# A copy moved from VectorE to ScalarE, and a row maximum issued two key tiles sooner, in an attention kernel

## The chip, the cores and the metric

The kernel runs on one core of a Trainium2 chip. The metric is the device time of one execution in microseconds. Before the change it is 3565.64 us, the median of three runs (3565.61 to 3567.53).

The engines go by short names: PE is TensorE's matrix multiplication and PEld its loading of weights, DVE is VectorE, ACT is ScalarE, POOL is GpSimd, and SP is SyncE, which here issues nearly all DMAs. A bank is one of the eight banks of PSUM, each 128 partitions by 512 fp32 values.

## The reference

Two layers, one after the other and with the same weights. Each layer is an attention block and a block of dense layers, both on a layer-normalised input and added back to it:

```python
def _A_ref(x, wqkv, wo):           # B = 1, S = 2048, D = 640, H = 32, Dh = 20
    qkv = (x @ wqkv).reshape(B, S, 3, H, Dh).transpose(2, 0, 3, 1, 4)
    q, k, v = qkv[0], qkv[1], qkv[2]
    scores = jnp.einsum("bhqd,bhkd->bhqk", q, k) * (Dh ** -0.5)
    p = _softmax(scores, axis=-1)
    o = jnp.einsum("bhqk,bhkd->bhqd", p, v)
    return o.transpose(0, 2, 1, 3).reshape(B, S, D) @ wo
...
x = x + _A_ref(_layernorm(x, axis=-1), A_wqkv, A_wo)
x = x + _B_ref(_layernorm(x, axis=-1), B_w1, B_b1, B_w2, B_b2)   # squared relu of x @ w1 + b1, times w2, + b2
```

The second pair of lines is repeated once. The change touches the softmax over the 2048 keys (its maximum) and the product with the values.

## The kernel before

A layer is three stages: the projections to queries, keys and values (`qkv`), the attention (`attention`), and the output projection with the dense layers. The change lies in the attention.

**Blocks and tiles.** The 32 heads form 8 groups of four, the 2048 queries four parts of 512. A group and a part make a block `t`, 32 blocks to a layer (`NBLK`), numbered from 0. For a block, the keys are gone through in 16 key tiles of 128 (`NKT`). For each key tile and head, `score` (L582) multiplies the keys with the 512 queries into a bank (L591), and ACT takes the exponential into SBUF (L598). `pv` (L600) then multiplies the four heads' exponentials with the values (L603) and adds the result up in bank 7 over the block's 16 tiles. The values carry a column of ones, so the sum of the exponentials comes out beside the result.

**The maximum.** The exponential needs each query's maximum over all keys beforehand. So the scores are also computed the other way round, queries on the partitions, for a later block: `smax` (L489) multiplies 128 queries of one head with 512 keys (L481), and DVE reduces the bank to one column of a small tile `mx` (L493). `smax_half` (L506) does it for two heads at once with 256 keys each: it writes one half of a bank for one head and, after a one-element memset `done_t` on DVE (L512) that serves as a mark, the other half for the other head; DVE reduces both at once (L516). The two halves of the 512 keys go to two columns of `mx`, `c` and `c + 4`, so that a block treated in this way has eight columns for each head and each 128 queries. `two_columns` (L500) has POOL fill the last four with a very small number first, as not every set of keys is done in halves.

When all maxima of block `t` are there (`t` is in the set `over`), `mrows_max` (L549) reduces the columns to one negated maximum (L551), `mrows` (L559) transposes it on DVE (L562), splits it in two parts on POOL (L271 and L276) and stores these to HBM by two DMAs (`d_m`); `mrows_load` (L569) reads them by two DMAs into two extra rows of the query tile `q_t[t]`, so that the score matmul subtracts the maximum.

**The order of the work** is written out by hand. `ORDERS` (L984) holds strings of letters; for nearly all of the attention it is `ubmbanawV` for each key tile: `a` and `b` are score matmuls of even and odd heads (two of each to a tile, in four banks that take turns), `m` and `n` maxima by 512 keys, `u` and `w` the two writes of a bank in halves, `V` the product with the values, for the tile before the one whose scores the string has just issued. Maxima take banks 4, 5 and 6 in turn. Each engine works through its instructions in the order in which `op` (L1088) issues them. So on PE, `w` waits for the mark of `u`, and `V` stands behind `w`; on DVE each tile has the mark, the reductions of `m` and `n`, and then that of `w`. What is issued right after `V` stands behind `w`'s reduction on DVE, and on ACT behind the four exponentials of the scores that were just issued.

`V` of the last tile of a block (tile 15) calls `finish` (L611): DVE copies bank 7 to SBUF (L616), four DMAs store the sums to HBM (`d_s`), and later steps, spread over the next block's tiles by `split`, load them again (`few`), take the reciprocals on POOL (L647), spread them by DMA (`d_r`), multiply and split the result on POOL (L658, L271, L276) and store it. The next block's first `V` starts bank 7 anew and must wait for the copy.

Each `V` also looks whether the next block's maximum is due (L1134): it must be in `over`, its queries must be loaded, and `state["begun"]`, the number of the key tile whose scores were last begun, must have come to `(t - 2) * NKT + 4`. That is the `V` of tile 3, two blocks before the block that needs it. The two loads follow when `begun` is two tiles further. Near the end of an attention the maxima become complete later than that, and the block's maximum is issued when they are.

In the last block no maxima are left, and `both_heads` (L1139) takes the exponentials of two heads in one instruction of 1024 columns (L1160).

Of the kernel before, what the change touches and what calls it, by code (L numbers as in the profile page):

```python
# [8 lines left out]
F32 = mybir.dt.float32  # L9
# [7 lines left out]
P = 128  # L17
# [10 lines left out]
NKT = S // P  # L28
# [5 lines left out]
NBLK = NG * NQB  # L34
# [5 lines left out]
def tile_layers(  # L40
# [11 lines left out]
    nc = tc.nc  # L52
# [3 lines left out]
    small = ctx.enter_context(tc.tile_pool(name="small", bufs=4))  # L56
# [6 lines left out]
    def name(p):  # L63
        n_alloc[0] += 1
        return f"{p}{n_alloc[0]}"

    def slot(shape, dtype, label):
        return arena.tile(shape, dtype, tag="slot", name=name(label))

    def dma(eng, dst, src):  # L70

        if dst.dtype == F32R:
            dst = dst.bitcast(F32)
        if src.dtype == F32R:
            src = src.bitcast(F32)
        eng.dma_start(dst, src)  # L76
# [177 lines left out]
    def split_to(dst_hi, dst_lo, src):  # L254

        nc.scalar.copy(dst_hi, src)
        nc.vector.tensor_sub(dst_lo, src, dst_hi.bitcast(F32))
# [12 lines left out]
    def pool_hi(dst, src):  # L270
        nc.gpsimd.tensor_copy(dst, src)  # L271
# [31 lines left out]
    def after(later, earlier, reason="one half of the rows adds to the bank that the other half has left"):  # L303
        tc.add_manual_dep(
            later.ins,
            earlier.ins.name,
            mybir.DependencyInfo(mybir.DependencyClass.Sync, mybir.DependencyReason.DATA),
            reason=reason,
        )
# [113 lines left out]
    k_t, q_t, v_t, mx_t, kept = {}, {}, {}, {}, {}  # L423
# [46 lines left out]

    def maxima(t):
        if t not in mx_t:
            mx_t[t] = small.tile([P, 4, 4, 8], F32, tag="mx", bufs=14, name=name("mx"))
            if t in PARTLY:
                nc.vector.memset(mx_t[t][:, :, :, :4], LEAST)
        return mx_t[t]

    def by_queries(dst, t, p, sub, c, par, keys=slice(0, QB)):

        b = 64 * par  # L480
        return nc.tensor.matmul(  # L481
            dst,
            q_t[t][b : b + 60, p, sub * P : (sub + 1) * P],
            k_t[t // NQB, c][b : b + 60, p, keys],
            start=True,
            stop=True,
        )
# [6 lines left out]
            maxima(t)[:, 2 * par + p, sub, c : c + 1], dst, axis=AX.X, op=ALU.max  # L494
        )

    halved = set()
    done_t = cpool.tile([1, 1], F32, name="done_t")

    def two_columns(t):  # L500

        if t not in halved:
            halved.add(t)
            nc.gpsimd.memset(maxima(t)[:, :, :, 4:], LEAST)

    def smax_half(bank, t, p, sub, c, half, par, earlier=None):  # L506

        w = QB // 2
        dst = bank[:, par * w : (par + 1) * w]
        m = by_queries(dst, t, p, sub, c, par, slice(half * w, (half + 1) * w))  # L510
        if earlier is None:
            mark = nc.vector.memset(done_t, 0.0)  # L512
            after(mark, m)
            return mark
        after(m, earlier, "matmuls on two halves of the rows write to one bank in turn")
        nc.vector.tensor_reduce(  # L516
            maxima(t)[:, p : p + 3 : 2, sub, c + 4 * half],
            bank.rearrange("q (r k) -> q r k", r=2),
            axis=AX.X,
            op=ALU.max,  # L520
        )
# [27 lines left out]
    def mrows_max(t):  # L549
        nm = nms[t % 2]  # L550
        nc.vector.tensor_reduce(  # L551
            nm[:, :16].rearrange("p (h s) -> p h s", h=4),
            mx_t.pop(t)[:, :, :, : 8 if t in halved else 4],
            axis=AX.X,
            op=ALU.max,
            negate=True,
        )
# [53 lines left out]
    def finish(t, acc):  # L611


        g, qb = divmod(t, NQB)
        o = slot([P, 2, QB], F32, "o")
        nc.vector.tensor_copy(o[:, 0, :], acc)  # L616
        res = []

        def store(q):
            ot = res.pop().rearrange("p l t -> p (l t)")  # L620
            for h in range(4):
                r0 = (4 * g + h) * DH
                dma(q, d_o[r0 : r0 + DH, qb], ot[32 * h : 32 * h + DH])

        if t == NBLK - 1:

            def invert():
                dst = ps_all("rs")
                nc.tensor.matmul(dst, sums_t, o[:, 0, :], start=True, stop=True)
                nc.vector.reciprocal(o[:, 1, :], dst)  # L630

            def divide():
                nc.vector.tensor_mul(o[:, 0, :], o[:, 0, :], o[:, 1, :])
                res.append(slot([P, 2, QB], F32R, "ot"))
                split_to(res[0][:, 0, :], res[0][:, 1, :], o[:, 0, :])

            return [invert, divide, lambda: store(nc.scalar)]

        few = small.tile([P, 16], F32, tag="few", bufs=2, name=name("few"))
        for h in range(4):  # L640
            dma(nc.sync, d_s[t, h : h + 1], o[32 * h + DH : 32 * h + DH + 1, 0, :])

        def load():
            dma(nc.sync, few, d_s[t].rearrange("h (q j) -> (h q) j", j=16))

        def invert():
            nc.gpsimd.tensor_tensor(few, few, minus_t, op=ALU.pow)  # L647

        def spread():
            dma(nc.sync, d_r[t].rearrange("h (q j) -> (h q) j", j=16), few)  # L650

        def gather():
            for h in range(4):
                dma(nc.sync, o[32 * h : 32 * h + 32, 1, :], d_r[t, h].partition_broadcast(32))

        def divide():
            ot = slot([P, 2, QB], F32R, "ot")
            nc.gpsimd.tensor_mul(o[:, 0, :], o[:, 0, :], o[:, 1, :])  # L658
            pool_hi(ot[:, 0, :], o[:, 0, :])
            pool_lo(ot[:, 1, :], o[:, 0, :], ot[:, 0, :].bitcast(F32))  # L660
            res.append(ot)

        return [load, invert, spread, gather, divide, lambda: store(nc.sync)]
# [328 lines left out]
    def attention(first, x_src, first_rows):  # L992
# [7 lines left out]
        state = {"begun": -1, "done": 0, "acc": None, "debt": 0}  # L1000
# [22 lines left out]
        over = {t for t in range(NBLK) if t not in ends and t not in done}  # L1023
# [64 lines left out]
        def op(o):  # L1088
            if o in "ab":
                par = "ab".index(o)  # L1090
                i, p = divmod(st_n[par], 2)
                if i >= last:
                    return
                st_n[par] += 1
                if i > state["begun"]:
                    state["begun"] = i
                    begin(i)
                score(i // NKT, i % NKT, 2 * p + par, es_of.setdefault(i, {}))
            elif o in "mn":
                par = "mn".index(o)  # L1100
                if full[par] or next_pair(full):
                    x = full[par].pop(0)
                    smax(sm_ring, *x, par)
                    turn.append(turn.pop(0))
                    did(x[0])
            elif o == "u":
                if parts or next_pair(parts):
                    x = parts.pop(0)
                    bank = turn.pop(0)
                    opened.append((bank, x, smax_half(banks[:, bank, :], *x, 0)))  # L1110
            elif o == "w":
                if opened:
                    bank, x, mark = opened.pop()
                    smax_half(banks[:, bank, :], *x, 1, mark)
                    turn.append(bank)
                    did(x[0])
            else:
                i = state["done"]
                if i >= last or i < last - NKT and min(st_n) < 2 * (i + 1):
                    return  # L1120
                t, u = divmod(i, NKT)
                if u == 0:
                    state["acc"] = banks[:, 7, :]
                pv(state["acc"], t, u, es_of.pop(i))
                state["done"] += 1
                if u == NKT - 1:
                    steps = finish(t, state["acc"])
                    split.update((i + j, f) for j, f in zip((4, 6, 7, 9, 11, 12), steps))
                t = rows["next"]
                if rows["at"] is not None:  # L1130
                    if state["begun"] >= rows["at"]:
                        mrows_load(t)
                        rows.update(next=t + 1, at=None)
                elif t in over and t in q_t and state["begun"] >= (t - 2) * NKT + 4:  # L1134
                    mrows_max(t)
                    mrows(t)
                    rows["at"] = state["begun"] + 2
# [39 lines left out]
        for o in "abab":  # L1177
            op(o)
# [376 lines left out]
```

## Time and profile before

| what | us |
|---|---|
| median of the three runs | 3565.64 |
| the profiled execution itself | 3565.74 |
| its span, first to last instruction | 3563.6 |
| attention of the first layer, first to last product with the values | 312.8 to 1384.8 |
| attention of the second layer | 2083.7 to 3156.1 |
| PE busy | 3543.9 |
| DVE busy | 2789.1 |
| ACT busy | 2626.9 |

The granted clock of TensorE is 1.000 for the whole span. A row of the timeline gives the start and the length in us, the engine, the line, the operation, what it writes and reads with the shapes, and how many such instructions in sequence the row sums up; in brackets stands the idle time of that engine just before, with what ended it. An instruction on DVE or ACT starts before the one ahead has quite ended, so the time from start to start is shorter than the length. A group's row ends with its total, the mean length in ns, and the idle time before it by what ended it. The stretch of a few tiles around the end of block 8 of the first layer is taken as the example throughout.

### The profile page before, as it was taken

The page shows a single profiled execution, that of the slowest core. Times are in us where ns is not written, and L with a number is a line of the kernel's source. Part 1 is how long each engine was busy: PE and PEld are TensorE (multiplying, and loading weights), DVE is VectorE, ACT ScalarE, POOL GpSimd, SP SyncE. Part 2 cuts the span into 40 slices and gives each one's busy share as a digit, 9 for nine tenths or more (in the row PEclk, how much of TensorE's full clock was granted, in tenths as well). Part 3 has the DMA queues.
Part 4 walks back from the last instruction along what each step waited for, and adds up shares of the span by engine and source line. Part 5 has one row for each costly group of instructions (what it writes and reads, how often), then busy time and mean ns, then how long its engine had stood idle before and what let it go on. Part 6 is the DMA issues. An engine that isn't in the chain of part 4 may idle for free.

```text
span 3563.6 us, 70654 instructions
## 1 busy us (share of the span) xinstructions
PE 3543.9 (99%) x26544; PEld 2153.9 (60%) x26544; DVE 2789.1 (78%) x6069; ACT 2626.9 (74%) x5146; POOL 811.2 (23%) x927
## 2 busy tenths in 40 slices
PE   9999999999999999999999999999999999999999
PEld 7896444444444446999988964444444444469998
DVE  8878999999999993455567789999999999924443
ACT  3778999999999995122237789999999999942221
POOL 6531444211211211111153201211211211211110
PEclk9999999999999999999999999999999999999999
DMA  9775555323211136734487652232232111366221
GB/s 307 273 233 167 170 157 157 105 70 81 57 46 51 46 103 207 255 103 113 135 272 246 197 150 71 62 82 62 64 81 56 50 45 40 116 218 244 74 82 37
DMA packets 377412, 452.76 MB, mean 127 GB/s; under 512 B 176642, under 2 KB 223746, under 8 KB 377070
## 3 DMA queue, kind: packets, MB, share of 16 engines
q1 hardware_dynamic: 376254, 445.89, 41.2%
q8 instruction: 208, 3.41, 0.4%
q10 hardware_dynamic: 816, 2.36, 0.2%
q14 instruction: 134, 1.10, 0.1%
HBM read 273.83 MB, written 174.30 MB: 126 GB/s over the span
## 4 chain that ended last, share of the span: by engine, by line
PE 91%; DVE 5%; DMA 1%; issue 1%; ACT 1%; POOL 0%; SPq 0%; DVEq 0%; ACTq 0%; POOLq 0%
PE banks L603 26%; PE banks L481 22%; PE banks L293 13%; PE banks L591 11%; PE banks L1321 9%; PE banks L331 9%; DVE mx L493 2%; DVE mx L516 1%; DVE o L616 1%; DMA q<-d_qk 1%; SPq L76 0%; DVE bst L244 0%; ACT e L598 0%; PE banks L1153 0%; ACT e L1160 0%
## 5 line engine op out<-in xcount | busy, mean ns | idle before, releaser
L598 ACT ACTIVATE e<-banks 128x512 f32<-128x512 f32 x3968 | 2028.3, 602 | 64.2 <-PE banks L591 46.6
L493 DVE TENSOR_REDUCE mx<-banks 128x1 f32<-128x512 f32 x2092 | 1344.4, 686 | 151.3 <-PE banks L481 83.9
L481 PE MATMUL banks<-k,q 60*128 60x512 f32 x4570 | 1392.7, 382 | 8.2 <-DVE v L377 1.7
L481 PEld LDWEIGHTS banks<-k,q 60*128 60x128 f32 x4570 | 703.2, 184 | 1000.1 <-DVE mx L493 824.9
L603 PE MATMUL banks<-e,vg 128*32 128x512 f32 x8192 | 1091.0, 605 | 1.5 <-ACT e L1160 1.5
L591 PE MATMUL banks<-q,k 62*128 62x512 f32 x3968 | 1091.3, 424 | 0.4 <-DVE mx L536 0.4
L516 DVE TENSOR_REDUCE mx<-banks 128x2 f32<-128x512 f32 x984 | 671.5, 682 | 1.3 <-PE banks L591 1.3
L591 PEld LDWEIGHTS banks<-q,k 62*128 62x128 f32 x3968 | 586.5, 184 | 8.5 <-ACT e L598 7.4
L536 DVE CUSTOM_DVE_ANT_0 rl<-banks,rl 128x512 f32<-128x512 f32 x510 | 332.8, 689 | 101.3 <-PE banks L481 91.0
L1306 ACT ACTIVATE r<-banks,b_t 128x512 f32<-128x512 f32 x96 | 66.2, 689 | 425.0 <-PE banks L293 401.2
L331 PE MATMUL banks<-xnT,wqk 64*128 64x512 f32 x2400 | 378.9, 394 | 0.3 <-ACT mark_t L333 0.3
L528 ACT ACTIVATE rl<-banks 128x512 f32<-128x512 f32 x510 | 270.8, 597 | 98.5 <-PE banks L481 88.3
L1321 PE MATMUL banks<-w,h 128*128 128x320 f32 x2304 | 340.4, 309 | 0.0
L1321 PEld LDWEIGHTS banks<-w,h 128*128 128x128 f32 x2304 | 339.2, 188 | 1.2
L293 PE MATMUL banks<-xnT,w 128*128 128x512 f32 x1440 | 329.4, 389 | 0.0
L603 PEld LDWEIGHTS banks<-e,vg 128*32 128x32 f32 x8192 | 161.1, 108 | 242.2 <-issue 221.8
L331 PEld LDWEIGHTS banks<-xnT,wqk 64*128 64x128 f32 x2400 | 285.2, 185 | 36.1 <-issue 2.4
L293 PEld LDWEIGHTS banks<-xnT,w 128*128 128x128 f32 x1440 | 269.6, 188 | 55.3
L271 POOL CAST mr<-nt 128x32 fp32r<-128x32 f32 x64 | 13.5, 211 | 1103.2 <-DVE done_t L512 1022.5
L647 POOL TENSOR_TENSOR few<-few,minus_t 128x16 f32<-128x16 f32 x62 | 179.9, 2902 | 210.6 <-DMA few<-d_s 209.0
L331 PE MATMUL banks<-wv,xnT 64*128 64x320 f32 x1920 | 199.5, 307 | 0.9 <-ACT mark_t L333 0.9
L331 PEld LDWEIGHTS banks<-wv,xnT 64*128 64x128 f32 x1920 | 187.2, 185 | 2.5 <-ACT mark_t L333 1.4
(89 smaller groups left out, 2158.3 us busy)
## 6 DMA issues: line engine op xcount, KB each, us to landing
q<-d_qk SPq DMA_DIRECT2D x242, 240.0 KB
d_qk<-ev SPq DMA_DIRECT2D x80, 512.0 KB
k<-d_qk SPq DMA_DIRECT2D x152, 240.0 KB
x<-d_x SPq DMA_DIRECT2D x84, 320.0 KB
d_qk<-ev SPq DMA_DIRECT2D x80, 256.0 KB
d_o<-ot SPq DMA_DIRECT2D x248, 80.0 KB
ot<-d_o SPq DMA_DIRECT2D x38, 512.0 KB
d_v<-v SPq DMA_DIRECT2D x32, 512.0 KB
```

Source lines behind the costliest of these rows:

```text
L293: nc.tensor.matmul(dst, a, b, start=(n == 0), stop=(n == last))
L331: m = nc.tensor.matmul(ch["dst"][:, :width], *pair, start=first, stop=last)
L481: return nc.tensor.matmul(dst, q_t[t][b : b + 60, p, sub * P : (sub + 1) * P], k_t[t // NQB, c][b : b + 60, p, keys], start=True, stop=True,)
L493: nc.vector.tensor_reduce(maxima(t)[:, 2 * par + p, sub, c : c + 1], dst, axis=AX.X, op=ALU.max)
L516: nc.vector.tensor_reduce(maxima(t)[:, p : p + 3 : 2, sub, c + 4 * half], bank.rearrange("q (r k) -> q r k", r=2), axis=AX.X, op=ALU.max,)
L528: nc.scalar.activation(res, dst, AF.Relu)
L536: nc.vector.tensor_tensor_reduce(out=r, in0=dst, in1=r, scale=1.0, scalar=LEAST, op0=ALU.add, op1=ALU.max, accum_out=maxima(t)[:, 2 * par ...
L591: nc.tensor.matmul(dst, k_t[t // NQB, kt // 4][b : b + 62, p, (kt % 4) * P : (kt % 4 + 1) * P], q_t[t][b : b + 62, p, :], start=True, stop ...
L598: nc.scalar.activation(es[p][:, par, :], dst, AF.Exp, scale=SCALE)
L603: nc.tensor.matmul(acc[32 * h : 32 * h + 32, :], v_t[t // NQB, kt // 8][:, kt % 8, 32 * h : 32 * h + 32], es[p][:, par, :], start=(kt == 0 ...
L647: nc.gpsimd.tensor_tensor(few, few, minus_t, op=ALU.pow)
L1321: nc.tensor.matmul(dst[:, :HALF], hs[f][:, hx, i * P : (i + 1) * P], w_2.piece(at_2(f0 + f, hw, hf)), start=(f == 0 and (hx, hw) == THREE[0]),
```

## The change

Three edits. The copy of a block's results out of bank 7 is done by ACT, but for the last block of a layer. The tile `mx` has six columns instead of eight: the first half of the keys still goes to column `c`, the second half to the next free one of columns 4 and 5, counted for each block, head and 128 queries by a new function `column`; the memset of POOL and the reduction of the columns become that much smaller. The maximum, its transposition and what follows from it are issued once `begun` has come to `(t - 2) * NKT + 2`, which is the `V` of tile 1; the loads, two tiles after, move with it.

```diff
-            mx_t[t] = small.tile([P, 4, 4, 8], F32, tag="mx", bufs=14, name=name("mx"))
+            mx_t[t] = small.tile([P, 4, 4, 6], F32, tag="mx", bufs=14, name=name("mx"))
...
-    halved = set()
+    halved = {}
...
         if t not in halved:
-            halved.add(t)
+            halved[t] = True
             nc.gpsimd.memset(maxima(t)[:, :, :, 4:], LEAST)
+
+    def column(*x):
+
+        halved[x] = halved.get(x, 3) + 1
+        assert halved[x] < 6
+        return halved[x]
...
-            maxima(t)[:, p : p + 3 : 2, sub, c + 4 * half],
+            maxima(t)[:, p : p + 3 : 2, sub, c if not half else column(t, p, sub)],
...
-            mx_t.pop(t)[:, :, :, : 8 if t in halved else 4],
+            mx_t.pop(t)[:, :, :, : 6 if t in halved else 4],
...
-        nc.vector.tensor_copy(o[:, 0, :], acc)
+        (nc.vector.tensor_copy if t == NBLK - 1 else nc.scalar.copy)(o[:, 0, :], acc)
...
-                elif t in over and t in q_t and state["begun"] >= (t - 2) * NKT + 4:
+                elif t in over and t in q_t and state["begun"] >= (t - 2) * NKT + 2:
```

## The prediction

> **What bounds the kernel now.** I read the page first: shares of the engines, the chain of waits, the groups.
>
> ```profile
> PE 3543.9 (99%) x26544; PEld 2153.9 (60%) x26544; DVE 2789.1 (78%) x6069; ACT 2626.9 (74%) x5146; POOL 811.2 (23%) x927
> ...
> PE 91%; DVE 5%; DMA 1%; issue 1%; ACT 1%; POOL 0%; SPq 0%; DVEq 0%; ACTq 0%; POOLq 0%
> ...
> L598 ACT ACTIVATE e<-banks 128x512 f32<-128x512 f32 x3968 | 2028.3, 602 | 64.2 <-PE banks L591 46.6
> ...
> L616 DVE COPY o<-banks 128x512 f32<-128x512 f32 x64 | 43.6, 681 | 72.1 <-PE banks L603 72.1
> L271 POOL CAST mr<-nt 128x32 fp32r<-128x32 f32 x64 | 13.5, 211 | 1103.2 <-DVE done_t L512 1022.5
> ```
>
> PE carries 91% of the chain, but the chain passes to DVE in places. The table of stages, over 300 us inside an attention (columns: length, then busy us of PE, PEld, DVE, ACT, POOL), shows why: three engines are nearly full at once.
>
> ```profile
> 600.00:900.00 300.00, 299.41 (x2281) 125.52 (x2277) 280.36 (x597) 291.00 (x570) 69.50 (x77) 1.00 0.33 90
> ```
>
> So I read the order of time around the end of a block. PE first; each L603 row is the eight matmul records of one key tile's product with the values (I call it V).
>
> ```profile
> 609.26 1.06 PE L603 MATMUL banks<-e,vg 128*32 128x512 f32 x8
> ...
> 611.36 1.06 PE L603 MATMUL banks<-e,vg 128*32 128x512 f32 x8
> ...
> 613.04 0.39 PE L591 MATMUL banks<-q,k 62*128 62x512 f32 x1
> ...
> 613.39 1.06 PE L603 MATMUL banks<-e,vg 128*32 128x512 f32 x8
> ...
> 615.88 1.06 PE L603 MATMUL banks<-e,vg 128*32 128x512 f32 x8
> ...
> 617.90 1.06 PE L603 MATMUL banks<-e,vg 128*32 128x512 f32 x8
> ```
>
> Ordinary key tiles alternate: 611.36 - 609.26 = 2.10 us, 613.39 - 611.36 = 2.03 us. The tile after the last V of a block (613.39, I call it V(15)) takes 615.88 - 613.39 = 2.49 us, where the alternation has 2.10 due: **a stall of 0.39 us at each block end**. DVE, then PE's weight load of the second half of the keys (L481, `w`):
>
> ```profile
> 614.21 0.68 DVE L516 TENSOR_REDUCE mx<-banks 128x2 f32<-128x512 f32 x1
> 614.81 0.68 DVE L616 COPY o<-banks 128x512 f32<-128x512 f32 x1
> ...
> 615.43 0.06 DVE L512 MEMSET done_t<- 1x1 f32 x1
> ```
> ```profile
> 615.57 0.18 PEld L481 LDWEIGHTS banks<-k,q 60*128 60x128 f32 x1 [0.38 <-DVE done_t L512]
> ```
>
> The copy takes a place of 0.60 us in DVE's queue (614.21 to 614.81 is what one reduction takes there). The mark `done_t` behind it comes late, `w` waits 0.38 us for the mark, and V waits behind `w`. The maximum over the columns and its transposition do the same four tiles on, after V(3):
>
> ```profile
> 622.04 1.06 PE L603 MATMUL banks<-e,vg 128*32 128x512 f32 x8
> ...
> 624.38 1.06 PE L603 MATMUL banks<-e,vg 128*32 128x512 f32 x8
> ```
> ```profile
> 623.46 0.28 DVE L551 TENSOR_REDUCE nm<-mx 128x16 f32<-128x128 f32 x1
> 623.78 0.21 DVE L562 STREAM_TRANSPOSE nt<-nm 128x32 f32<-128x32 f32 x1
> ```
> ```profile
> 624.06 0.18 PEld L481 LDWEIGHTS banks<-k,q 60*128 60x128 f32 x1 [0.22 <-DVE done_t L512]
> ```
>
> That tile takes 2.34 us, **a stall of 0.24 us**. A block of 16 tiles pays 0.63 us in these two places.
>
> **The copy, taken off DVE.** In each attention the copies of blocks 0 to 29 meet maxima on DVE; that of block 30 falls into the last block, which has none, and that of block 31 stays on DVE. 2 x 30 x 0.39 = -23.4 us.
>
> **The copy, put on ACT.** It is queued behind the four exponentials of the next key tile, and ahead of the four after these. ACT there:
>
> ```profile
> 613.86 1.10 ACT L598 ACTIVATE e<-banks 128x512 f32<-128x512 f32 x2
> ...
> 614.34 1.18 ACT L598 ACTIVATE e<-banks 128x512 f32<-128x512 f32 x2
> ...
> 617.41 2.07 ACT L598 ACTIVATE e<-banks 128x512 f32<-128x512 f32 x4 [0.43 <-PE banks L591]
> ```
> ```profile
> 53.00 0.59 ACT L263 COPY r<-banks 128x512 f32<-128x512 f32 x1 [1.23 <-PE banks L331]
> 53.48 0.59 ACT L265 CAST ev<-banks 128x512 fp32r<-128x512 f32 x1
> ```
>
> Four exponentials back to back take 2.07 us, so they start (2.07 - 0.60) / 3 = 0.49 us apart. A copy of this very shape from a bank, by ACT, holds the next instruction off 0.48 us and takes 0.59. The fourth exponential starts at 614.34, the next one today at 614.34 + 1.18 - 0.60 = 614.92, so 0.58 later and not 0.49: ACT has 0.09 us free there. The copy would start at 614.83 (V(15) has ended by 613.39 + 1.06 = 614.45, and today's copy never waits for its slot: all idle time ahead of L616 on the page is PE's), end at 615.42, and let the next exponential start at 615.31, 0.39 us late.
>
> Who waits for that? First the next V, which overwrites the copied bank: due at 613.39 + 2.10 = 615.49, after 615.42, so just free. Then the scores, which rotate over four banks. The last score matmul of a tile needs the bank of the last exponential of the tile before:
>
> ```profile
> 614.95 0.18 PEld L481 LDWEIGHTS banks<-k,q 60*128 60x128 f32 x1 [0.15 <-DVE mx L516]
> 615.01 0.18 PEld L591 LDWEIGHTS banks<-q,k 62*128 62x128 f32 x1
> ```
> ```profile
> 612.90 0.18 PEld L591 LDWEIGHTS banks<-q,k 62*128 62x128 f32 x1
> ```
>
> Its weights load at 615.01, 0.05 us after that exponential's end (613.86 + 1.10 = 614.96): ACT already gates it. The matmul itself follows 613.04 - 612.90 = 0.14 us later, and that is all the slack. With the copy the four exponentials end at 615.31 + 2.07 = 617.38, the weights come at 617.43, and the matmul was due 613.04 - 611.36 = 1.68 us after V, at 615.49 + 1.68 = 617.17. **A new stall of 0.26 us, in the tile after V(0).** ACT wins its delay back there at once, since it works back to back while PE stands. Bounds: 0, if the rotation hides the delay, and 0.65, if nothing on ACT overlaps (worked out below). I take 0.26, from the rows of the same tiles: 60 x 0.26 = +15.6 us.
>
> The Trainium skill, ScalarE: Activation LUTs, What ACT_TABLE_LOAD costs, gives 186 ns + 0.833 ns an element for an activation with immediate scale, and an overlap of 93 ns back to back: an estimate of 0.52 us between starts where the rows above show 0.49. By it the stall would be 0.43 us and the time 10 us above my forecast; the measured spacing decides.
>
> The copy in the last block meets wide exponentials that run without a gap:
>
> ```profile
> 3125.99 29.59 ACT L1160 ACTIVATE e<-banks 128x1024 f32<-128x1024 f32 x32
> ```
>
> There it lies on ACT's path in full: 2 x 0.49 = +1.0 us.
>
> **The maximum, two tiles sooner.** It moves only where its turn, and not its columns, holds it back:
>
> ```profile
> 1120.65 0.68 DVE L616 COPY o<-banks 128x512 f32<-128x512 f32 x1
> ...
> 1129.30 0.28 DVE L551 TENSOR_REDUCE nm<-mx 128x16 f32<-128x128 f32 x1
> ...
> 1154.36 0.68 DVE L616 COPY o<-banks 128x512 f32<-128x512 f32 x1
> ...
> 1171.40 0.29 DVE L551 TENSOR_REDUCE nm<-mx 128x16 f32<-128x128 f32 x1
> ```
>
> From the first blocks on it stands 8.65 us after the copy (623.46 - 614.81), as at 1129.30 in block 24; in block 25 it is 17 us behind, waiting for maxima. So 25 in each attention move, from V(3) to V(1). There it lands behind the tile with ACT's new stall. In that tile the matmuls that DVE reduces first come on time (the stall is at PE's last score, behind `m` and `n`), so DVE gains 0.26 us on PE, and the maximum's delay of 0.22 to 0.24 us fits in: the stalls overlap instead of adding. 50 x 0.24 = -12.0 us. A rest may show one tile on, through the reductions behind it: 0 to 0.1 us a block, taken as 0.05, +2.5 us. If ACT's stall is not there, the cover is gone and the 0.24 is paid at V(1).
>
> On the queues, the two stores of the rows and, two tiles later, their two loads move past the load of the sums:
>
> ```profile
> 618.14 0.34 SPq L76 DMA_DIRECT2D few<-d_s  x1
> 624.29 1.10 SPq L76 DMA_DIRECT2D d_m<-mr  x2
> ```
>
> That load now waits on SP behind the stores, until about 624.29 - 4.1 + 1.1 = 621.3, 3 us later. POOL's two instructions on the rows stand ahead of its reciprocal already, and POOL sat 1022.5 us waiting for DVE in front of them; and the divided results are read again only after the attention stage, whose last two blocks have no maximum behind their copies. I cost this at nothing; without that cover it would be one delay of 3 us at the end of an attention, 6 us in all.
>
> **Six columns.** The reduction took 278 ns over 128 elements and 209 over 64:
>
> ```profile
> L551 DVE TENSOR_REDUCE nm<-mx 128x16 f32<-128x128 f32 x47 | 13.0, 278 | 0.3
> ...
> L551 DVE TENSOR_REDUCE nm<-mx 128x16 f32<-128x64 f32 x17 | 3.6, 209 | 0.0
> ```
>
> So about 1.1 ns an element, 35 ns less for 96. It counts only in the ten blocks whose maximum isn't covered: -0.4 us. POOL's smaller memset lies in POOL's idle time.
>
> **Sum**: -23.4 + 15.6 + 1.0 - 12.0 + 2.5 - 0.4 = -16.7 us. The profiled execution took 3565.74 us (span 3563.6), 0.1 above the median of the runs; 3549 by either.
>
> **The rivals.** *The stalls add*: DVE's head start is lost before V(1), and the maximum still costs 0.24 less 0.035, about 0.2 us: the -12.0 and +2.5 become 50 x -0.035 = -1.8, the sum -9.0: 3557. It is also the time if the move doesn't happen. For it: today's stall at V(15) leaves nothing to V(3).
> *ACT's delay is hidden*: score and V never wait; then the maximum is paid (-1.8): -23.4 + 1.0 - 1.8 - 0.4 = -24.6, 3541. Against it: the 0.05 us gate in two different tiles.
> *Slower: ACT overlaps nothing at the copy.* The copy has waits of its own (today DVE's queue shows 118 of them for 64 copies, 50 ns in the middle):
>
> ```profile
> L616 DVEq EVENT_SEMAPHORE  x118: 21/50/29212, 377.9 to 3127.5; - x118
> ```
>
> If ACT takes them, the copy and the next exponential one after the other, then from 614.96: 0.10 for two waits, 0.59, 0.05, so the exponential starts at 615.70, its four end at 617.77, the last score's weights come at 617.82, and the stall is 0.65 us: 60 x 0.65 = 39.0 in place of 15.6, 3572. It turns slower from 0.54 us on. Against it: a copy that starts 0.48 us before its follower, with 0.59 us of its own.
>
> **How the numbers follow.** A run can tell from no change about 0.2%, 7 us. Forecast 50% (3543 to 3557 by itself: the ACT stall at 0.20 to 0.35, as its six steps are read to 0.01 us, the rest at 0 to 0.1), adding stalls 20%, hidden delay 14%, slower 10%, and 6% for no effect that I can name. The first three are faster; a quarter of the second may fall within 0.2%. The slower rival lies half on either side of the bound, the last 6% likewise within or above: faster 0.79, same 0.14, slower 0.07. The range takes in the first three cases: 3538 to 3559.
>
> **What would show it.** The tile after V(15) back at 2.03 to 2.10 us; the one after V(0) at about 2.3, its last L591 weights 0.05 us behind an exponential that follows a copy; the one after V(3) at 2.10; the maximum some 4.1 us sooner. A long tile after V(1) means the stalls add; a next V that waits for ACT's copy means that bank 7 is handed over late, which I hold to be just free.

## The result, and the profile after

The changed kernel takes 3546.81 us (median of four runs, 3545.72 to 3547.86), the kernel before, run beside it, 3565.62 us (3565.01 to 3567.53). The ratio is 0.9946, with a 95% interval of 0.9929 to 0.9964: 18.8 us less, where 16.7 were forecast. The profiled execution took 3545.72 us, its span is 3543.3.

Line numbers are those of the changed kernel: its score matmul is L597, the exponential L604, the product with the values (V) L609, the copy L622, the reduction over the columns L557, the transposition L568 and the mark `done_t` L518. From the page of its profile, the busy times and the chain of waits:

```profile
PE 3528.8 (100%) x26544; PEld 2151.1 (61%) x26544; DVE 2758.7 (78%) x6007; ACT 2645.4 (75%) x5208; POOL 810.5 (23%) x927
...
PE 96%; DVE 1%; DMA 1%; issue 1%; ACT 0%; POOL 0%; SPq 0%; DVEq 0%; ACTq 0%
```

DVE's share of the chain has gone from 5% to 1%, and ACT's is no larger for it. The V rows of PE's timeline around the end of block 8, the stretch that the prediction worked with:

```profile
610.95 1.07 PE L609 MATMUL banks<-e,vg 128*32 128x512 f32 x8
...
612.97 1.06 PE L609 MATMUL banks<-e,vg 128*32 128x512 f32 x8
...
615.37 1.07 PE L609 MATMUL banks<-e,vg 128*32 128x512 f32 x8
...
617.38 1.06 PE L609 MATMUL banks<-e,vg 128*32 128x512 f32 x8
...
619.51 1.06 PE L609 MATMUL banks<-e,vg 128*32 128x512 f32 x8
...
621.53 1.07 PE L609 MATMUL banks<-e,vg 128*32 128x512 f32 x8
```

V(15) starts at 610.95, V(0) at 612.97, V(3) at 619.51. The tile after V(15) takes 2.02 us, where it took 2.49. The tile after V(0), from 612.97 to 615.37, takes 2.40, and it is the only long one: the tiles after it go on with 2.01 and 2.13, and the one after V(3), with 2.02, is ordinary too. As the alternation stands, that tile had 2.11 due, so one stall of 0.28 to 0.29 us has come in the place of two of 0.39 and 0.24. (Why ordinary tiles alternate between 2.02 and 2.11 us was not tried. A stall's size read from one tile leans on that pattern; the lengths of whole blocks, below, don't.)

ACT in the same stretch, then the weight loads of PE, then DVE:

```profile
612.30 0.62 ACT L622 COPY o<-banks 128x512 f32<-128x512 f32 x1
612.76 4.08 ACT L604 ACTIVATE e<-banks 128x512 f32<-128x512 f32 x8
```
```profile
614.45 0.18 PEld L597 LDWEIGHTS banks<-q,k 62*128 62x128 f32 x1 [0.19 <-ACT e L604]
...
614.94 0.18 PEld L597 LDWEIGHTS banks<-q,k 62*128 62x128 f32 x1 [0.21 <-ACT e L604]
```
```profile
615.83 0.68 DVE L522 TENSOR_REDUCE mx<-banks 128x2 f32<-128x512 f32 x1
616.43 0.24 DVE L557 TENSOR_REDUCE nm<-mx 128x16 f32<-128x96 f32 x1
616.77 0.21 DVE L568 STREAM_TRANSPOSE nt<-nm 128x32 f32<-128x32 f32 x1
```

The copy holds ACT for 0.46 us (612.30 to 612.76), and then ACT works without a gap. The last score's weights come at 614.94, the one before's at 614.45, both released by an exponential. The maximum runs at 616.43, behind the next tile's reductions, and V(2) at 617.38 shows nothing of it.

Over a whole attention, the first and the last V (starts of the weight loads, as groups of one line, the kernel before in the first fence, the changed one in the second):

```profile
L603 PEld LDWEIGHTS banks<-e,vg x4096: 106/108/109, 312.8 to 1384.3; 128*32 128x32 f32 x196
```
```profile
L609 PEld LDWEIGHTS banks<-e,vg x4096: 106/108/109, 312.7 to 1375.4; 128*32 128x32 f32 x196
...
L609 PEld LDWEIGHTS banks<-e,vg x4096: 106/108/109, 2072.9 to 3135.3; 128*32 128x32 f32 x196
```

The first attention goes from 1071.5 to 1062.7 us, the second from 1072.0 (2083.7 to 3155.7) to 1062.4: together 18.4 us. From the starts of all V rows, blocks 1 to 24 take 33.35 us each on average, where they took 33.70.

### The profile page after: what moved, and what is told of

The parts are those of the page before. It is cut to its first block, busy times and chain, and to the rows that moved or that the text cites. A ratio compares the mean times of both kernels' runs of the same rounds, so it can differ in the third digit from the quotient of the medians.

```text
span 3543.3 us, 70757 instructions
## 1 busy us (share of the span) xinstructions
PE 3528.8 (100%) x26544; PEld 2151.1 (61%) x26544; DVE 2758.7 (78%) x6007; ACT 2645.4 (75%) x5208; POOL 810.5 (23%) x927
## 4 chain that ended last, share of the span: by engine, by line
PE 96%; DVE 1%; DMA 1%; issue 1%; ACT 0%; POOL 0%; SPq 0%; DVEq 0%; ACTq 0%
PE banks L609 28%; PE banks L481 22%; PE banks L293 13%; PE banks L597 13%; PE banks L1327 10%; PE banks L331 9%; DMA q<-d_qk 1%; PE banks L1159 0%; ACT e L1166 0%; DVE bst L244 0%; DVE mx L493 0%; SPq L76 0%; DVE xnT L257 0%; DVE x L252 0%; DMA d_qk<-ev 0%
## 5 line engine op out<-in xcount | busy, mean ns | idle before, releaser
L604 ACT ACTIVATE e<-banks 128x512 f32<-128x512 f32 x3968 | 2026.6, 612 | 27.2 <-PE banks L597 4.4
L481 PE MATMUL banks<-k,q 60*128 60x512 f32 x4570 | 1375.9, 381 | 2.9 <-DVE v L377 1.7
L597 PE MATMUL banks<-q,k 62*128 62x512 f32 x3968 | 1112.8, 427 | 0.4 <-DVE mx L542 0.4
L609 PE MATMUL banks<-e,vg 128*32 128x512 f32 x8192 | 1091.0, 605 | 1.5 <-ACT e L1166 1.5
L597 PEld LDWEIGHTS banks<-q,k 62*128 62x128 f32 x3968 | 590.3, 184 | 33.4 <-ACT e L604 31.3
L609 PEld LDWEIGHTS banks<-e,vg 128*32 128x32 f32 x8192 | 161.1, 108 | 251.0 <-issue 227.2
L653 POOL TENSOR_TENSOR few<-few,minus_t 128x16 f32<-128x16 f32 x62 | 179.9, 2902 | 360.5 <-DMA few<-d_s 352.4
```

The lines of the kernel that those rows point to most:

```text
L481: return nc.tensor.matmul(dst, q_t[t][b : b + 60, p, sub * P : (sub + 1) * P], k_t[t // NQB, c][b : b + 60, p, keys], start=True, stop=True,)
L597: nc.tensor.matmul(dst, k_t[t // NQB, kt // 4][b : b + 62, p, (kt % 4) * P : (kt % 4 + 1) * P], q_t[t][b : b + 62, p, :], start=True, stop ...
L604: nc.scalar.activation(es[p][:, par, :], dst, AF.Exp, scale=SCALE)
L609: nc.tensor.matmul(acc[32 * h : 32 * h + 32, :], v_t[t // NQB, kt // 8][:, kt % 8, 32 * h : 32 * h + 32], es[p][:, par, :], start=(kt == 0 ...
```

## The experiments

The theory was that two stalls per block have become one: ACT is late by the copy and holds up PE's last score in the tile after V(0), and DVE's maximum costs nothing as long as it lies behind that stall. The rivals were that ACT's delay is hidden, that the earlier place is good by itself, and that the stalls merely add and the gain is the copy's alone. Each run below was timed against the kernel before, on the same chip.

### The copy on ACT alone

```diff
-        nc.vector.tensor_copy(o[:, 0, :], acc)
+        (nc.vector.tensor_copy if t == NBLK - 1 else nc.scalar.copy)(o[:, 0, :], acc)
```

> The kernel before with one edit: the copy of a block's results on ACT. Theory (the copy's delay on ACT holds up the last score of the tile after V(0), and DVE's maximum costs its own 0.24 us unless it lies behind that stall): of 0.63 us a block, 0.39 goes, 0.28 comes in the tile after V(0) and 0.24 stays in the tile after V(3), so 60 x 0.11 less and 1.0 more for the last blocks: about 3560 us. Rival (ACT's delay is hidden, and the long tile after V(0) in the changed kernel is the maximum's): the 23 us go in full, about 3543 us, and the tile after V(0) is 2.03 to 2.10 us.

Measured: 3558.35 us, ratio 0.9978 (0.9969 to 0.9988). V rows of this kernel around a block end, from V(15) to V(4):

```profile
612.22 1.06 PE L603 MATMUL banks<-e,vg 128*32 128x512 f32 x8
614.32 1.06 PE L603 MATMUL banks<-e,vg 128*32 128x512 f32 x8
616.71 1.07 PE L603 MATMUL banks<-e,vg 128*32 128x512 f32 x8
618.71 1.07 PE L603 MATMUL banks<-e,vg 128*32 128x512 f32 x8
620.84 1.07 PE L603 MATMUL banks<-e,vg 128*32 128x512 f32 x8
623.15 1.06 PE L603 MATMUL banks<-e,vg 128*32 128x512 f32 x8
```

The tile after V(15), from 612.22, is back at 2.10 us. The tile after V(0), from 614.32, takes 2.39, and the one after V(3), from 620.84, takes 2.31, where 2.02 or so was due after the 2.13 ahead of it (its median over blocks 2 to 24 is 2.25). Both stalls are there, and blocks 1 to 24 take 33.59 us on average. ACT's delay isn't hidden, and this edit alone brings 8 of the 19 us.

### The maximum sooner, alone

```diff
-                elif t in over and t in q_t and state["begun"] >= (t - 2) * NKT + 4:
+                elif t in over and t in q_t and state["begun"] >= (t - 2) * NKT + 2:
```

> The kernel before with one edit: the maximum due at V(1) instead of V(3); copy on DVE, eight columns. Theory: nothing covers it there, the 0.39 us after V(15) stay and the 0.24 us move from the tile after V(3) to the tile after V(1): 3565.6 us, no change (within 3 us). Rival (the earlier place is a better one by itself): up to 50 x 0.24 = 12 us less, about 3554 us.

Measured: 3566.08 us, ratio 0.9999 (0.9990 to 1.0008). The weight loads of `w` after V(15) and after V(1), at one block end of the second attention:

```profile
2117.53 0.18 PEld L481 LDWEIGHTS banks<-k,q 60*128 60x128 f32 x1 [0.38 <-DVE done_t L512]
...
2121.89 0.18 PEld L481 LDWEIGHTS banks<-k,q 60*128 60x128 f32 x1 [0.22 <-DVE done_t L512]
```

The same two waits as before the change, 0.38 and 0.22 us, the second two tiles sooner. The earlier place is worth nothing by itself. With the run before: the copy alone brings 7.9 us and the move alone nothing, but the changed kernel has 18.8, so some 11 us come from the two being together (the columns, below, are worth 33 ns in each of 47 uncovered maxima, about 1.5).

### Six columns, alone and left out

```diff
-            mx_t[t] = small.tile([P, 4, 4, 8], F32, tag="mx", bufs=14, name=name("mx"))
+            mx_t[t] = small.tile([P, 4, 4, 6], F32, tag="mx", bufs=14, name=name("mx"))
...
-            maxima(t)[:, p : p + 3 : 2, sub, c + 4 * half],
+            maxima(t)[:, p : p + 3 : 2, sub, c if not half else column(t, p, sub)],
```

> The kernel before with one edit: six columns instead of eight; copy on DVE, maximum at V(3). Theory: 35 ns less in each uncovered maximum over columns, 47 of them: about 3564 us, and the tile after V(3) at 2.32 us where it was 2.36. Rival (DVE has that time anyway): 3565.6 us and 2.36 us.

Measured: 3564.81 us, ratio 0.9997 (0.9987 to 1.0006). The time can't tell this kernel from the one before, the rows can:

```profile
L557 DVE TENSOR_REDUCE nm<-mx 128x16 f32<-128x96 f32 x47 | 11.5, 245 | 0.3
```

The reduction takes 245 ns instead of 278, and the tile after V(3) has a median of 2.32 us where it had 2.35. The other way round, the changed kernel with this edit undone:

> The changed kernel with eight columns: copy on ACT and maximum at V(1) alone. Theory (the maximum lies in time that DVE has): no difference in 48 blocks, 0.4 us in the late ones, 3547 us and 2.39 us for the tile after V(0), 2.02 for the next. Rival (the head start is used up to the last, so that 35 ns count in each block): 1.7 us more, and one of the tiles after V(0), V(1), V(2) 0.03 us longer.

Measured: 3547.38 us, ratio 0.9949 (0.9935 to 0.9962). Blocks 1 to 24 take 33.36 us with eight columns and 33.35 with six. Behind ACT's stall the 33 ns are free.

### The maximum one tile later, and one tile sooner

```diff
-                elif t in over and t in q_t and state["begun"] >= (t - 2) * NKT + 2:
+                elif t in over and t in q_t and state["begun"] >= (t - 2) * NKT + 3:
```

> The changed kernel with the maximum due at V(2), one tile later. Theory (ACT's stall gives DVE a head start, which is lost little by little): the maximum's 0.2 us comes back in part, 0 to 0.1 us a block, 3547 to 3552 us. Rival (only the very next tile covers it, the stalls add elsewhere): 48 x 0.2 = 10 us more, about 3557 us.

Measured: 3557.83 us, ratio 0.9976 (0.9967 to 0.9985), and 33.59 us for blocks 1 to 24, as with the copy alone: the rival's time. Here the theory failed in a part: the head start of DVE isn't lost little by little but at once. DVE in this kernel, from the tile that ACT stretches (V(0) at 614.35, V(1) at 616.75):

```profile
617.21 0.68 DVE L522 TENSOR_REDUCE mx<-banks 128x2 f32<-128x512 f32 x1
618.18 0.06 DVE L518 MEMSET done_t<- 1x1 f32 x1 [0.29 <-PE banks L481]
618.39 1.29 DVE L493 TENSOR_REDUCE mx<-banks 128x1 f32<-128x512 f32 x2 [0.16 <-PE banks L481]
...
620.20 0.24 DVE L557 TENSOR_REDUCE nm<-mx 128x16 f32<-128x96 f32 x1
```

After V(1) DVE idles 0.29 us, waiting for PE's `u`. DVE can't work ahead: each of its reductions needs a matmul of PE's present tile. So what PE's stall gives DVE is one gap, in front of the next tile's mark, and one tile on DVE is again as late as ever. Over the whole run, the table of waits (us in total, times, longest) shows that gap; first the changed kernel, then the one with the maximum a tile later, then the one with the copy alone:

```profile
DVE done_t L518 <- PE banks L481: 4.3, 13, 0.6
```
```profile
DVE done_t L518 <- PE banks L481: 19.0, 62, 0.8
```
```profile
DVE done_t L512 <- PE banks L481: 18.3, 61, 0.6
```

61 and 62 times about 0.3 us, once for each copy that ACT does; in the changed kernel the maximum fills it.

One tile sooner (`+ 1`), in the stretched tile itself:

> The changed kernel with the maximum due at V(0), one tile sooner, in the very tile that ACT's copy stretches. Theory: PE's `w` waits for the later of two, its mark on DVE (0.2 us late) and its turn behind the last score (0.28 us late), so the two overlap there as well: 3547 us, within 3. Rival (the stalls add): 48 x 0.2 = 10 us more, about 3557 us.

Measured: 3546.68 us, ratio 0.9948 (0.9936 to 0.9961), and 33.36 us for blocks 1 to 24. Its V rows, from V(0) at 613.01:

```profile
613.01 1.06 PE L609 MATMUL banks<-e,vg 128*32 128x512 f32 x8
615.40 1.07 PE L609 MATMUL banks<-e,vg 128*32 128x512 f32 x8
617.42 1.06 PE L609 MATMUL banks<-e,vg 128*32 128x512 f32 x8
```

As in the changed kernel: 2.39 and 2.02 us. In this tile PE waits for ACT at the last score and for DVE's mark at `w`, both at once: the mark ends at 614.99, the last score's weights come at 614.98 and those of `w` at 615.07. So there are two good places, the stretched tile and the one after it. In the third (V(2), the run above) and the fifth tile (V(3), the copy alone) the maximum is paid for.

### The cover's size: the maximum twice

```diff
-        nc.vector.tensor_reduce(
-            nm[:, :16].rearrange("p (h s) -> p h s", h=4),
-            mx_t.pop(t)[:, :, :, : 6 if t in halved else 4],
+        mx = mx_t.pop(t)
+        for _ in range(2):
+            nc.vector.tensor_reduce(
+                nm[:, :16].rearrange("p (h s) -> p h s", h=4),
+                mx[:, :, :, : 6 if t in halved else 4],
```

> The changed kernel with the reduction over the columns done twice in a row. Theory (ACT's stall of 0.28 us is the whole cover, and of the maximum's 0.45 us on DVE some 0.2 reach PE when uncovered): with 0.25 to 0.35 us more the mark comes 0.45 to 0.55 us late, 0.17 to 0.27 us of it beyond the cover, 50 times: 9 to 14 us more, 3556 to 3561 us, in the tile after V(1). Rival (DVE has far more time behind ACT's stall): 3547 to 3549 us.

Measured: 3562.27 us, ratio 0.9990 (0.9981 to 0.9999), 15 us above the changed kernel. DVE and V rows of one block:

```profile
618.95 0.53 DVE L559 TENSOR_REDUCE nm<-mx 128x16 f32<-128x96 f32 x2
```
```profile
617.89 1.06 PE L611 MATMUL banks<-e,vg 128*32 128x512 f32 x8
620.18 1.06 PE L611 MATMUL banks<-e,vg 128*32 128x512 f32 x8
```

The pair takes 0.53 us where one takes 0.24, and the tile after V(1) goes from 2.01 to 2.29 us. Blocks 1 to 24 are 0.23 us longer on average, so of the 0.29 us added some 0.06 are still covered and the rest shows. The maximum as it is nearly uses the cover up; the 33 ns of the eight columns, above, still fit in. The expectation left out that the late blocks, which have no cover, pay for the second reduction too.

### The copy twice

```diff
         (nc.vector.tensor_copy if t == NBLK - 1 else nc.scalar.copy)(o[:, 0, :], acc)
+        if t < NBLK - 1:
+            nc.scalar.copy(o[:, 0, :], acc)
```

> The changed kernel with the copy on ACT done twice in a row, for the blocks that ACT copies. Theory (the stall is ACT's queue: whatever it is given there comes out at PE less a fixed slack): 60 x 0.48 = 29 us more and 1 us more for the last blocks, about 3577 us. As the second copy ends 0.48 us later, part of it shows in the tile after V(15), whose next V waits for the copied bank, and the sum of the two tiles grows by 0.48 us. Rival (ACT has the time, 2 us free in each block, and the stall has another cause): 3547 to 3552 us.

Measured: 3586.63 us, ratio 1.0057 (1.0042 to 1.0072), 40 us above the changed kernel and not 30. ACT at one block end, and V(0):

```profile
617.47 0.62 ACT L622 COPY o<-banks 128x512 f32<-128x512 f32 x1
618.12 0.59 ACT L624 COPY o<-banks 128x512 f32<-128x512 f32 x1
618.60 0.60 ACT L604 ACTIVATE e<-banks 128x512 f32<-128x512 f32 x1
```
```profile
618.75 1.06 PE L609 MATMUL banks<-e,vg 128*32 128x512 f32 x8 [0.55 <-ACT o L624]
```

The second copy starts only after the first one's end: 0.65 us from start to start instead of 0.48. It writes where the first does, which may be the reason; no run here gives it another place to write. 60 times 0.65 is 39 us, and the two attentions are 39 us longer. V(0) now waits for the copied bank, as expected: it starts 0.04 us after the second copy's end (618.12 + 0.59 = 618.71). What ACT is given at this place beyond the one copy comes out at PE nearly in full: 0.62 us a block.

### Two ways to get more

PE has `w` to do while the last score waits for ACT. In the second tile of each string of eight, the two were exchanged:

```diff
-        12: "ubmbanawV" * 8,
+        12: "ubmbanawV" + "ubmbanwaV" + "ubmbanawV" * 6,
```

> The changed kernel with the last score and `w` exchanged in the second tile of each string of eight tiles, so in the tile after V(0), and in the one after V(8), where nothing is held up. Theory (PE stands idle in front of the last score, waiting for ACT): `w`, 0.14 us of PE, is done in that time, and 60 x 0.14 = 8 us go: about 3538 us. Rival (the mark of `w` on DVE is late as well, or V waits for the score alone with nothing to fill the gap): 3547 us, or up to 0.1 us a block slower, 3553 us.

Measured: 3546.76 us, ratio 0.9946 (0.9933 to 0.9958); the changed kernel, timed again beside it:

> The changed kernel as it is, to be compared with the three others of this set on the same chip: 3547 us.

It took 3547.43 us, ratio 0.9947 (0.9935 to 0.9960). No gain. PE's rows of the stretched tile with the exchange:

```profile
614.77 0.61 PE L481 MATMUL banks<-k,q 60*128 60x512 f32 x2
615.15 0.50 PE L597 MATMUL banks<-q,k 62*128 62x512 f32 x1
615.58 1.06 PE L609 MATMUL banks<-e,vg 128*32 128x512 f32 x8
```

V starts 0.43 us after the late score. In the changed kernel, too, it is 0.43 (614.94 to 615.37): there `w`, which works on the other half of the rows, starts beside the score and takes no time of its own:

```profile
614.94 0.50 PE L597 MATMUL banks<-q,k 62*128 62x512 f32 x1
614.94 0.38 PE L481 MATMUL banks<-k,q 60*128 60x256 f32 x1
```

The theory had counted it as a step behind the score.

The second way looks after the ends of the attentions. It is meant to make a maximum that becomes complete after V(1) wait for the next block's V(0) or V(1) where that is early enough, and it sends block 30's copy, among the wide exponentials, back to DVE:

```diff
-        (nc.vector.tensor_copy if t == NBLK - 1 else nc.scalar.copy)(o[:, 0, :], acc)
+        (nc.vector.tensor_copy if t >= NBLK - 2 else nc.scalar.copy)(o[:, 0, :], acc)
...
-                elif t in over and t in q_t and state["begun"] >= (t - 2) * NKT + 2:
+                elif (
+                    t in over
+                    and t in q_t
+                    and state["begun"] >= (t - 2) * NKT + 2
+                    and (state["begun"] % NKT in (1, 2) or state["begun"] >= (t - 1) * NKT + 3)
+                ):
```

> The changed kernel with two edits for its end: a maximum that becomes complete later in a block than V(1) waits for V(0) or V(1) of the next block, if that is early enough (two in each attention), and the copy of block 30, which falls among the wide exponentials, is back on DVE. Theory (a place behind ACT's stall costs nothing, and the wide exponentials leave ACT no time): 4 x 0.24 and 2 x 0.4 us less, about 2 us under the changed kernel, 3545 us, to be seen in the blocks' lengths (33.35 instead of 33.74 us for blocks 25 and 26, the last block 0.4 us shorter). Rival (the late maxima then hold something else up): blocks 26 and 27 over 33.4 us.

Measured: 3545.27 us (3544.49 to 3548.70), ratio 0.9945 (0.9932 to 0.9959). V(0) of blocks 25 and 26 of the first attention, first in the changed kernel, then in this one:

```profile
1146.66 0.64 PE L609 MATMUL banks<-e,vg 128*32 128x512 f32 x4
...
1180.40 0.64 PE L609 MATMUL banks<-e,vg 128*32 128x512 f32 x4
```
```profile
1147.02 0.64 PE L609 MATMUL banks<-e,vg 128*32 128x512 f32 x4
...
1180.38 0.64 PE L609 MATMUL banks<-e,vg 128*32 128x512 f32 x4
```

Block 25 takes 33.36 us instead of 33.74. The two attentions are 1061.4 and 1061.7 us long, about 2 us less together than in the changed kernel. As a whole time that lies within the spread of the runs; by its two attentions it is the shortest of the kernels here.

The edit does more than it was meant to. Only one maximum is under way at a time, and already the one that the changed kernel issues behind V(3) of block 0 is held back to block 1; all that follow move on with it. In the trace every maximum from block 1 to block 27 of an attention stands behind a V(0), as here in block 9, and those that the changed kernel issues behind V(1) come 15 tiles later:

```profile
614.64 0.24 DVE L557 TENSOR_REDUCE nm<-mx 128x16 f32<-128x96 f32 x1
```

That is the place of the run with one tile sooner, and as good: 33.36 us for blocks 1 to 24. So this run tests the pair of both, the late ones covered and all the others at V(0).

## Why the prediction was right

**The copy, off DVE** (-23.4 us). Right: the tile after V(15) is back in the alternation.

**The gate of ACT**, which the prediction read off two tiles, is nearly everywhere. In the kernel before, the last score's weights come 0.05 us after the end of the last exponential of the tile ahead, whose bank the score needs, in 671 of the 768 tiles of blocks 1 to 24 of both attentions; but for one, the others stand one tile behind the two stalls of DVE. In the tile after V(0) they came 0.28 to 0.40 us after that end, which was slack for ACT, left by DVE's stall. With the copy off DVE that slack is gone, just where ACT's copy strikes: in the changed kernel it is 0.05 us in all 768. So ACT is a limit of the ordinary tiles too, although the chain of waits gives it 1% before and 0% after.

**The copy, on ACT** (+15.6 us, a stall of 0.26 us in the tile after V(0)). Right in place, cause and nearly in size: 0.28 us. The last score's weights load at 614.94, and the fourth exponential behind the copy ends at 614.89. The same wait has grown from 7.4 to 31.3 us, first the kernel before, then the changed one, in the table of waits, with the wait of V's weights for the copy below it:

```profile
PEld banks L591 <- ACT e L598: 7.4, 14, 0.8
```
```profile
PEld banks L597 <- ACT e L604: 31.3, 130, 0.8
...
PEld banks L609 <- ACT o L622: 15.3, 61, 0.3
```

130 waits, not 60, since the score before the last is released by ACT as well (614.45 above), which the prediction had not seen. The next V was held to be just free of the copy, and is, with no slack left: the copy ends at 612.30 + 0.62 = 612.92, V starts at 612.97. The 61 waits of V's weights that the table puts down to the copy are 0.25 us each, which is the idle time of the weight load in front of any V; V follows `w` by 0.21 us there as in other tiles, so they cost nothing. The rival by which the copy's waits and its neighbours follow one another without overlap is out: from the copy's start to the next exponential's it is 0.46 us.

**The maximum two tiles sooner** (-12.0 us, and +2.5 for a rest). The overlap is right, and the runs with one edit alone and with other places show it: 0.24 us a block (33.59 against 33.35) where the maximum isn't in the stretched tile or the next. The rest of 0.05 us was put too high: with 33 ns more on DVE, in the run with eight columns, a block grows by 0.01. That is the main difference between 16.7 and 18.8 us. The count of 50 is two too high: in block 0, which has no copy ahead of it, the maximum stands behind V(3) in both kernels, so 24 in each attention move. The prediction's picture, DVE gaining 0.26 us on PE, is right for one tile only.

**The queues.** Right to cost nothing, though the delay on SP is real: the load of the sums is issued 8.11 us after V(15) starts, where it was 4.75, so 3.4 us later. POOL's reciprocals wait longer for them (`few<-d_s`), 352.4 us in all where it was 209.0; with the maximum sooner alone it is 352.5, with the copy alone 210.8, so this comes of the move. Nothing on the chain waits for POOL.

**Six columns** (-0.4 us) and **the last blocks** (+1.0 us). 33 ns instead of the estimated 35, and only where uncovered. The last blocks were put a little too high: the last block is 0.44 us longer in the first attention and 0.29 in the second (27.07 and 27.22 to 27.51 us between its first and last V), 0.7 in all.

**The sum**, by blocks: 48 blocks with 0.35 us less each make 16.8, the first blocks 0.7, blocks 25 to 29 another 2.2, and blocks 30 and 31 cost 1.3, which makes the 18.4 us of the two attentions. (Block 30 gets 0.3 us of that as the copy's stall now shows one block on.) The prediction's sum with 0.28 for the stall, 48 for the count, no rest and 0.7 for the last blocks would have been about 18 us. The profiled execution is 1.6 us shorter still than the attentions tell. The stretch between the two attentions, which the change doesn't touch, is 697.6 us there, 699.5 before and 697.6 to 701.2 in the traces of all kernels here, a spread wider than the difference.

## What to carry to other kernels

Where three engines are each nearly full, look for work on one that can fall into a stall of another: two stalls of 0.24 and 0.28 us cost 0.28 when they coincide, and here such a place was found by the period of the smallest repeated piece of work, not by busy shares (PE read 99% before and 100% after). An engine whose work comes from the stalled one keeps its head start only until it has caught up, here one tile, so the place must be right to a tile or two. Two edits that bring 8 us and nothing by themselves can bring 19 together, so try them as a pair before dropping one.

## What the runs showed of the hardware

Exponentials back to back last longer and longer while their starts stay 0.48 us apart. Single rows of ACT in the changed kernel, behind the copy:

```profile
612.76 0.65 ACT L604 ACTIVATE e<-banks 128x512 f32<-128x512 f32 x1
...
614.21 0.68 ACT L604 ACTIVATE e<-banks 128x512 f32<-128x512 f32 x1
...
615.64 0.72 ACT L604 ACTIVATE e<-banks 128x512 f32<-128x512 f32 x1
```

Their mean over the kernel was 0.60 us before. The last score's weights follow the end of the fourth (614.21 + 0.68 = 614.89) by 0.05 us, not the next one's start, so with 0.68 instead of 0.60 us it frees its bank 0.08 us later than the mean length says. Why they grow was not tried.

Two matmuls on different halves of the rows, one of them late, cost no more than the late one: exchanging them moved nothing, and V starts 0.43 us after the late one in both orders.
